# Attention and a SwiGLU FFN in one kernel: unit 2's transposes moved, a two-tile start of block 1, w_out loaded in thirds

## The chip, the cores and the metric

The kernel runs on one core of one Trainium2 chip. The metric is the device time of one execution in microseconds; lower is better. All profile times are microseconds from the start of the profiled span.

## The reference

Sliding-window attention with ALiBi biases on 8 batches, 8 heads, 576 positions and a head width of 64, followed by an FFN on the 4608 x 512 result:

```python
scores = scale * np.matmul(q, k.transpose(0, 1, 3, 2))
bias = slopes[:, None, None] * (-np.abs(rel).astype(np.float32))[None, :, :]
mask = (rel >= 0) & (rel < 128)
scores = np.where(mask, scores + bias[None], -1000000000.0)
attn = np.exp(scores - np.max(scores, axis=-1, keepdims=True))
attn = attn / (np.sum(attn, axis=-1, keepdims=True) + 1e-09)
x = np.matmul(attn, v)         # then heads side by side: (4608, 512)
g = x @ w_gate                 # (512, 1536)
silu = g * (1.0 / (1.0 + np.exp(-g)))
out = (silu * (x @ w_val)) @ w_out
```

## The kernel before

**Attention units.** Two batches form a superblock; each superblock has nine units of 128 rows, the ninth made of the last 64 rows of both. For a unit the kernel transposes the rows of q and k on TensorE (`transposed`; the names are `pt` for the PSUM tile, `kn` and `qn` for the loaded rows), computes transposed scores (`ps` at L282; `psc` at L318 for the narrow ones), takes the exponential on ACT (`ex`, `exc`), multiplies with a mask on DVE, and forms the weighted sums `av` with a column of ones beside v, which gives the denominators (L350). DVE then divides: a reciprocal `rec` (L353) and a product `x` (L354), in two halves of four heads. `x_transposed` turns x on TensorE into `px` (L377) and a copy takes it to `xT`, the FFN's moving operand: on DVE for units 0 to 3 (L379), on ACT later (L381). The transposes of the first units share one PSUM buffer, tag "po"; later ones use the four buffers of tag "a", which scores and sums use as well.

**FFN blocks.** Nine blocks of 512 rows, four units each (the last is made of the ninth units). For each of twelve groups m of 128 hidden columns, `wide` computes `pg` and `pv` (L403) in three PSUM buffers of tag "gv". `gate` makes `tt` on ACT (L421) and `uu` on DVE (L422); `val` makes `hT` on DVE (L433). `wide` can be begun on the first tiles of a block: `begin(n, tiles, block)` computes the first n products of a block on the columns that are there, and the later call does the rest. `project` multiplies block 0's `hT` with `wo_sb` (`po`, L457), from the last group, m = 11, down to m = 0, in four sets of twelve matmuls. From block 1 on the output product uses a seven-product scheme, for which DVE makes sums of w_out (`T`, L481 to L484) and of hT (`S`, L491 to L494).

**Order.** The first four units (`first_tiles`) and the first FFN steps are written out by hand for TensorE, DVE and ACT. After that a scheduler orders the instructions by priority and its own estimate of time, until step 60, when TensorE's order is fixed again; `tc.high_priority()` puts instructions ahead. Each engine executes its list in order. The passage from block 0 to block 1, where unit 6 is divided and transposed and scores for units 7 and 8 are made, lies in the scheduled part.

**Loads.** All loads but the first are issued on POOL in an order written out by hand at the end of the kernel. They cast from 32 to 16 bits. POOL's loads use eight completion semaphores in turn, so a load is issued once the load eight places earlier has landed. `load_qk` loads 128 KB for each of k and q, `load_v` 128 KB of v, in two halves of 64 KB for a ninth unit; `load_w(c0, c1)` loads 256 hidden columns of each of w_gate and w_val; wo_sb (12 x 128 rows of 512) is loaded in two halves, rows 6 to 11 first.

Of the kernel before, what the change touches and what calls it, by code (L numbers as in the profile page):

```python
# [50 lines left out]
def kernel(  # L51
# [10 lines left out]
    nc = tc.nc  # L62
# [127 lines left out]
    def load(rank):  # L190
        load_qk(rank)
        load_v(rank)
# [137 lines left out]
    def weighted(i):  # L330

        s, p = units[i]
        x = xpool.tile([P, H, D], FP16, name="x", tag="x")
        xs[i] = x
        for half in range(2):
            pool, tag = (ps_f, "gv") if i < FIRST else (ps_a, "a")
            av = pool.tile([P, 4, D + 1], FP32, name="av", tag=tag)
            todo = []
            for j in range(4):
                h = 4 * half + j  # L340
                if p == 8:
                    for n, kt in enumerate((3, 7, 8)):
                        todo.append((j, ex[(s, "c", n)][:, slot(h), :], va[9 * s + kt][:, h, :]))
                else:
                    if p not in (0, 4):
                        todo.append((j, ex[(s, p - 1)][:, slot(h), 128:256],
                                     va[9 * s + p - 1][:, h, :]))
                    todo.append((j, ex[(s, p)][:, slot(h), 0:128], va[9 * s + p][:, h, :]))
            for n, (j, w, val) in enumerate(todo):
                nc.tensor.matmul(av[:, j, :], w, val, start=(n == 0), stop=(n == len(todo) - 1))  # L350
            rec = xpool.tile([P, 4, 1], FP32, name="rec", tag="rec", bufs=4)
            with tc.high_priority() if i == 7 else ExitStack():
                nc.vector.reciprocal(rec, av[:, :, D:D + 1])  # L353
                nc.vector.tensor_mul(x[:, 4 * half:4 * half + 4, :], av[:, :, 0:D],  # L354
                                     rec.broadcast_to([P, 4, D]))
# [8 lines left out]
    def x_transposed(i):  # L364
        n, j = place(i)
        if n not in xT:
            xT[n] = bpool.tile([P, NKB, 512], FP16, name="xT", tag="xTc" if n == 8 else "xT",
                               bufs=1 if n == 8 else 3)
        x = xs.pop(i).rearrange("p h d -> p (h d)")
        dst = xT[n][:, :, j * P:(j + 1) * P]  # L370
        if i >= X_DMA_FROM:
            nc.sync.dma_start_transpose(dst, x)
            return
        pool, tag, n = (ps_f, "po", 1) if i < FIRST else (ps_a, "a", 4)
        pt = pool.tile([P, NKB, P], FP16, name="px", tag=tag, bufs=n)
        for kb in range(NKB):
            nc.tensor.transpose(pt[:, kb, :], x[:, kb * P:(kb + 1) * P], idm if i < FIRST else idm2)  # L377
        if i < FIRST:
            nc.vector.tensor_copy(dst, pt)  # L379
        else:  # L380
            nc.scalar.copy(dst, pt)  # L381
# [325 lines left out]
    def ffn():  # L707

        for n in range(NBLK):
            if n > 1:  # L710
                parts = chain(strassen(n - 1, 0), strassen(n - 1, 1))
            if n == 1:
                begin(3, 3, 1)
                for j in range(PRE):
                    for _ in project(0, j, ps_f, "po", 1):
                        yield 1.0
            if n == SEVEN_FROM:
                break
            due, given = 0, 0
            for m in range(NMB):  # L720
                for half, _ in enumerate(gate_val(n, m)):
                    scored[0] = False
                    yield 1.0
                    due += n > 1 and 2 * m + half in AT
                    while due and not (scored[0] and given % 7 == 1):
                        next(parts)
                        due, given = due - 1, given + 1
                        yield 0.75
                    if n > 1:
                        for _ in range(1 + (len(later) > 3)):  # L730
                            if later:
                                later.pop(0)()
                if n == 1:
                    if m in (4, 6, 8, 10):
                        for _ in project(0, m // 2 - 2, ps_f, "po", 1):
                            yield 1.0
                    if m in (4, 6, 8):
                        weight_sums(m // 2 - 2)
                if n > 0 and m >= 9:
                    (at_once if n == 1 and m < 11 else later.extend)(sums(n, m - 9))  # L740
                if n + 1 == SEVEN_FROM:
                    if m == SILU_AT:
                        attention_ends()
                        by_silu.update((n, i) for i in range(m + 1, NMB))
                    if m in (SILU_AT + 1, SILU_AT + 2):
                        later.extend(gate_val_weight_sums(m - SILU_AT - 1))
                    if m == SILU_AT:
                        later.extend(x_sums(n + 1))
            if n > 1:
                assert next(parts, 0) == 0  # L750
        ends = [strassen(NBLK - 1, t) for t in range(2)]
        tail = ExitStack()
        for n, k, name, which in seven_steps():
            if k == 0 and n > SEVEN_FROM:
                assert next(parts, 0) == 0
                parts = chain(strassen(n - 1, 0), strassen(n - 1, 1))
            if n == SEVEN_FROM and k in (1, 3, 10, 17):
                later.extend(gate_val_weight_sums(2 + (k + 4) // 7))
            yield 0.5
            if k % 3 == 2 and k < 42:  # L760
                next(parts)
                yield 0.75
            if k == 20 and n + 1 < NBLK:
                later.extend(x_sums(n + 1))
            if k == 35:
                later.extend(sums(n, 0))
            if name == "fourth" and which is not None and which[1] > 3:
                if n + 1 < NBLK or k < 39:
                    later.extend(sums(which[0], which[1] - 3))
            for _ in range(2 if len(later) > 4 or k < 7 else 1):  # L770
                if later:
                    later.pop(0)()
            if n == NBLK - 1 and k == 38:
                at_once(later)
                later.clear()
                tail.enter_context(tc.manual_schedule(engines={ET.DVE}))
            if n == NBLK - 1 and k == 39:
                one, two = sums(n, 1), sums(n, 2)
                one[0]()
            if n == NBLK - 1 and k == 41:  # L780
                one[1]()
                next(ends[0])
                yield 0.75
            if n == NBLK - 1 and k == 42:
                two[0]()
        assert next(parts, 0) == 0 and not later
        at_once((two[1], one[2], two[2], one[3], two[3]))

        for t in (1, 0, 1, 0, 1, 0, 1, 0, 0, 1, 0, 1, 1):
            next(ends[t])  # L790
            yield 0.75
        tail.close()
# [28 lines left out]
    def begin(n, tiles, block=0):  # L821

        for m, which in ((0, "g"), (0, "v"), (1, "g"), (1, "v"), (2, "g"), (2, "v"))[:n]:
            if early.get((block, m, which), (None, 0))[1] < tiles * P:
                wide(block, m, which, tiles * P)

    def first_tiles():

        first_masks()
        transposes_to(need[0])  # L830
        for n, _ in enumerate(run(scores(0))):
            if n == 0:
                transposes_to(need[1])
        for i in range(FIRST):
            if i + 1 < FIRST:
                for n, _ in enumerate(run(scores(i + 1))):
                    if n == 0 and i + 2 < FIRST:
                        transposes_to(need[i + 2])
            else:
                later_masks()  # L840
            weighted(i)
            if 0 < i < FIRST - 1:
                x_transposed(i - 1)
        begin(4, 2)
        x_transposed(2)
        x_transposed(3)
        begin(4, 3)

# [36 lines left out]
            nc.gpsimd.dma_start(dst[:, :, c0:c1], src[:, :, c0:c1])  # L885


    queue = ExitStack()
    queue.enter_context(tc.manual_schedule(engines={ET.Pool}))
    load_qk(1, "qk")  # L890
# [19 lines left out]
    load_qk(7, "qk")  # L910
    load_v(6)
    load_w(1280, 1536)
    load_v(7)
    load(8)
    load_qk(9)
    load_qk(10, "q")
    nc.gpsimd.dma_start(wo_sb[:, 6:12, :], wo2[:, 6:12, :])
    nc.gpsimd.dma_start(wo_sb[:, 0:6, :], wo2[:, 0:6, :])
    load_v(9)
    load_qk(10, "k")  # L920
    load_v(10)
# [94 lines left out]
```

The softmax here doesn't subtract the row's maximum and nothing guards it: scores larger than these inputs give would overflow.

## Time and profile before

| what | value |
|---|---|
| three timed runs | 338.82, 339.06, 339.23 us (median 339.06) |
| profiled run: device time, span of the core | 339.0 us, 337.2 us |
| TensorE matmuls / weight loads | 328.0 us / 217.8 us busy |
| DVE / ACT / POOL | 274.3 / 208.0 / 109.8 us busy |
| loads by POOL (q0) | 18.62 MB as written |
| granted TensorE clock | full throughout |

A busy time adds the stretches in which at least one instruction of the engine ran. In the timeline a row gives the start, the duration, the engine, the line, the operation with its operands and how many instructions were merged into the row; in brackets stands the idle time before it and what ended it. Rows named PEld are weight loads, which run beside matmuls. "DMA" in a bracket is a transfer that landed.

### The profile page before, as it was taken

How to read it: one execution, taken by the hardware profiler on the slowest of the kernel's cores; microseconds unless marked ns; L12 is line 12 of the kernel's file. 1: busy time of each engine (PE TensorE's matmuls, PEld its weight loads, DVE VectorE, ACT ScalarE, POOL GpSimd, SP SyncE). 2: the span in 40 equal slices, each digit the busy share in tenths (PEclk: the TensorE clock that was granted, in tenths of full speed). 3: DMA queues.
4: the chain of work that ended last, by engine and by line, in shares of the span. 5: the costliest groups of instructions: out<-in, count | busy, mean ns of one | idle time of the engine just before them, and what ended most of it. 6: DMA issues, size and time to landing. Idle time of an engine off the chain costs nothing.

```text
span 337.2 us, 7693 instructions
## 1 busy us (share of the span) xinstructions
PE 328.0 (97%) x2947; PEld 217.8 (65%) x2947; DVE 274.3 (81%) x643; ACT 208.0 (62%) x415; POOL 109.8 (33%) x136
## 2 busy tenths in 40 slices
PE   8999989999999999999999999999999999999994
PEld 4564445454455665656655655666788888888884
DVE  4668877998798679998899999999855885775683
ACT  4866775565675766656656557463467667776650
POOL 8977682295783372665217000000000000000000
PEclk9999999999999999999999999999999999999999
DMA  9999999999999999999999952031101101011014
GB/s 151 169 178 179 166 101 190 141 112 162 140 160 136 175 132 127 178 153 168 151 184 156 135 106 78 18 64 47 65 0 64 62 2 65 3 62 64 0 64 125
DMA packets 160037, 37.37 MB, mean 111 GB/s; under 512 B 147328, under 2 KB 155648, under 8 KB 160000
## 3 DMA queue, kind: packets, MB, share of 16 engines
q0 software_dynamic: 118336, 18.62, 87.7%
q1 hardware_dynamic: 40976, 17.64, 30.0%
q10 hardware_dynamic: 688, 0.62, 0.6%
q8 instruction: 23, 0.38, 0.5%
q14 instruction: 14, 0.11, 0.1%
HBM read 37.91 MB, written 9.44 MB: 140 GB/s over the span
## 4 chain that ended last, share of the span: by engine, by line
PE 83%; DMA 8%; DVE 3%; POOL 2%; ACT 1%; issue 1%; DVEq 0%; POOLq 0%
PE po L538 19%; PE pv L403 15%; PE pg L403 15%; PE gX L627 9%; PE gY L627 5%; PE av L350 4%; DMA wo_sb<-in_moe_w_out_dram 4%; PE ps L282 4%; PE p L538 3%; PE po L457 3%; DMA va<-in_v_dram 3%; PE gZ L627 2%; DMA qn<-in_q_dram 2%; PE px L377 1%; PE psc L318 1%
## 5 line engine op out<-in xcount | busy, mean ns | idle before, releaser
L403 PE MATMUL pv<-xT,wv_sb 128*128 128x512 f16 (+3 forms) x308 | 76.1, 365 | 1.0 <-DVE uu L422 0.9
L403 PE MATMUL pg<-xT,wg_sb 128*128 128x512 f16 (+3 forms) x312 | 76.0, 363 | 0.3 <-DVE xT L379 0.2
L421 ACT ACTIVATE tt<-pg 128x512 f16<-128x512 f32 x68 | 40.9, 603 | 46.7 <-PE pg L403 46.7
L288 ACT ACTIVATE ex<-ps 128x512 f16<-128x512 f32 x96 | 50.0, 606 | 7.6 <-PE ps L282 7.6
L422 DVE SCALAR_TENSOR_TENSOR uu<-tt,pg 128x512 f16<-128x512 f16 x67 | 45.5, 679 | 9.3 <-ACT tt L421 9.1
L433 DVE TENSOR_TENSOR hT<-uu,pv 128x512 f16<-128x512 f16 x68 | 46.1, 679 | 2.8 <-PE pv L403 1.3
L181 POOL DMA_DIRECT2D va<-in_v_dram x40 | 34.3, 862 | 32.3 <-PE av L350 22.6
L538 PEld LDWEIGHTS <-hT 128*128 128x128 f16 x384 | 37.2, 98 | 10.6 <-issue 0.8
L403 PEld LDWEIGHTS <-wv_sb 128*128 128x128 f16 x308 | 27.5, 98 | 25.0 <-issue 3.5
L403 PEld LDWEIGHTS <-wg_sb 128*128 128x128 f16 x312 | 27.8, 98 | 22.9 <-issue 1.9
L187 POOL DMA_DIRECT2D qn<-in_q_dram x39 | 33.4, 864 | 21.3 <-DMA va<-in_v_dram 9.8
L187 POOL DMA_DIRECT2D kn<-in_k_dram x39 | 33.5, 860 | 19.1 <-DMA qT<-qn 6.4
L538 PEld LDWEIGHTS <-S 128*128 128x128 f16 x288 | 27.4, 98 | 7.3 <-issue 1.4
L294 DVE TENSOR_TENSOR ex<-ex,m_reg 128x1024 f16<-128x1024 f16 x42 | 28.6, 684 | 2.4 <-ACT ex L288 2.3
L354 DVE TENSOR_TENSOR x<-av,rec 128x256 f16<-128x256 f32 x72 | 28.6, 418 | 0.4
L538 PE MATMUL po<-T,S 128*128 128x256 f16 x192 | 25.9, 273 | 0.3 <-ACT u2s L564 0.3
L538 PE MATMUL po<-T,hT 128*128 128x256 f16 x192 | 26.0, 272 | 0.0
L322 ACT ACTIVATE exc<-psc 128x512 f16<-128x512 f32 x40 | 21.3, 607 | 1.9 <-PE psc L318 1.9
L681 DVE TENSOR_TENSOR hT<-s,v 128x512 f16<-128x512 f16 x18 | 7.6, 423 | 17.7 <-ACT s L680 17.7
L350 PEld LDWEIGHTS <-ex 128*128 128x128 f16 x384 | 17.4, 97 | 4.1 <-issue 0.7
L350 PE MATMUL av<-va,ex 128*128 128x65 f16 x384 | 19.3, 193 | 0.1
L282 PE MATMUL ps<-qT,kT 64*128 64x256 f16 x192 | 16.9, 272 | 0.1
(130 smaller groups left out, 533.8 us busy)
## 6 DMA issues: line engine op xcount, KB each, us to landing
out_dram<-osb SPq DMA_DIRECT2D x32, 256.0 KB, 2.3
va<-in_v_dram POOLq DMA_DIRECT2D x32, 128.0 KB, 9.0
qn<-in_q_dram POOLq DMA_DIRECT2D x31, 128.0 KB, 8.2
kn<-in_k_dram POOLq DMA_DIRECT2D x31, 128.0 KB, 9.0
wg_sb<-in_moe_w_gate_dram POOLq DMA_DIRECT2D x6, 256.0 KB, 7.7
wv_sb<-in_moe_w_val_dram POOLq DMA_DIRECT2D x6, 256.0 KB, 8.3
wo_sb<-in_moe_w_out_dram POOLq DMA_DIRECT2D x2, 768.0 KB, 11.2
kn<-in_k_dram POOLq DMA_DIRECT2D x8, 64.0 KB, 8.1
```

The costliest lines, as they stand in the source:

```text
L181: nc.gpsimd.dma_start(va[rank][p0:p1, :, 0:D], src)
L187: nc.gpsimd.dma_start(t_[p0:p1], src)
L282: nc.tensor.matmul(two[par][:, j, :], kT[rows, ks, pair, :], qT[rows, p:p + 2, pair, :], start=(j == 0 and not early_tile), stop=(j == 1))
L288: nc.scalar.activation(e[:, o:o + 2, :], banks[q4][par], AF.Exp, scale=scale)
L294: nc.vector.tensor_mul(e[:, o, :], e[:, o, :], reg[:, o, :])
L350: nc.tensor.matmul(av[:, j, :], w, val, start=(n == 0), stop=(n == len(todo) - 1))
L403: nc.tensor.matmul(ps[:, c0:c1], w[:, kb, ms], xT[n][:, kb, c0:c1], start=(kb == 0 and c0 == 0), stop=(kb == NKB - 1 and c1 == 512), skip_ ...
L421: nc.scalar.activation(tt, pg[:, c0:c1], AF.Tanh, scale=0.5)
L422: nc.vector.scalar_tensor_tensor(out=uu, in0=tt, scalar=one if (n, m) == PIN else 1.0, in1=pg[:, c0:c1], op0=ALU.add, op1=ALU.mult)
L433: nc.vector.tensor_mul(hT[n][:, m, c0:c1], acted[(n, m)][1][:, c0:c1], pv[:, c0:c1])
L538: nc.tensor.matmul(dst, a[:, m, cols], b[:, m, :], start=(start and m == 0), stop=(m == HM - 1), skip_group_check=True)
L627: nc.tensor.matmul(dst[:, i, :], w[:, kb, c0 + i * P:c0 + (i + 1) * P], a[:, kb, :], start=(start and i == 0 and kb == 0), stop=(i == 1 an ...
```

## The change

Four edits, all of order:

1. In `first_tiles` the transposition of unit 2's x is put ahead of `begin(4, 2)`, the first FFN products of block 0; before, it followed them.
2. At the start of block 1, `begin(2, 2, 1)` is put ahead of `begin(3, 3, 1)`: the first pg and pv of block 1 are begun on two tiles (units 4 and 5), and continued on the third (unit 6) by the call after it.
3. The divisions of unit 6 get the priority that unit 7's have.
4. On POOL, wo_sb is loaded in three parts of four rows (8 to 11, 4 to 7, 0 to 3) instead of two of six, and rank 8 is loaded as k and q first, v later.

```diff
-            with tc.high_priority() if i == 7 else ExitStack():
+            with tc.high_priority() if i in (6, 7) else ExitStack():
                 nc.vector.reciprocal(rec, av[:, :, D:D + 1])
...
             if n == 1:
+                begin(2, 2, 1)
                 begin(3, 3, 1)
...
                 x_transposed(i - 1)
+        x_transposed(2)
         begin(4, 2)
-        x_transposed(2)
         x_transposed(3)
         begin(4, 3)
...
+    def load_wo(m0, m1):
+        nc.gpsimd.dma_start(wo_sb[:, m0:m1, :], wo2[:, m0:m1, :])
...
     load_w(1280, 1536)
+    load_qk(8)
+    load_wo(8, 12)
     load_v(7)
-    load(8)
+    load_wo(4, 8)
     load_qk(9)
     load_qk(10, "q")
-    nc.gpsimd.dma_start(wo_sb[:, 6:12, :], wo2[:, 6:12, :])
-    nc.gpsimd.dma_start(wo_sb[:, 0:6, :], wo2[:, 0:6, :])
+    load_v(8)
+    load_wo(0, 4)
     load_v(9)
     load_qk(10, "k")
     load_v(10)
```

In the built program, TensorE's order differs from the one before in two places only: at the edit in `first_tiles`, and from the passage between blocks 0 and 1 to the sums of unit 9. DVE's and ACT's differ from unit 6's divisions to the first sums S of block 1.

## The prediction

> **What bounds the kernel now.** I read the page first, then TensorE's timeline stretch by stretch, then the DVE timeline and the transfer rates where it has gaps. The page, and the chain of waits:
>
> ```profile
> PE 328.0 (97%) x2947; PEld 217.8 (65%) x2947; DVE 274.3 (81%) x643; ACT 208.0 (62%) x415; POOL 109.8 (33%) x136
> ...
> 45.58 13.21 DMA wo_sb<-in_moe_w_out_dram
> ```
>
> TensorE sets the end, but 97% hides gaps: ends of matmuls are modelled and overlap. I measure a gap as the distance between two starts less the streaming time, 0.216 us for 512 columns (four take 0.86 in the chain), 0.109 for 256, 0.055 for 128. So counted, TensorE idles some 14 us up to 105 us, and under 4 us after that, mostly the tail. Three places bear on the change.
>
> ```profile
> 18.91 0.39 PE L377 MATMUL px<-idm,x 128*128 128x128 f16 x4
> 19.82 0.38 PE L377 MATMUL px<-idm,x 128*128 128x128 f16 x4 [0.52 <-DVE xT L379]
> ...
> 31.78 0.23 PEld L214 LDWEIGHTS <-qn 128*128 128x128 f16 x4 [0.17 <-DMA qn<-in_q_dram]
> ```
>
> Place A: the transposes of units 2 and 3 share one PSUM buffer ("po"), so the second waits for the first one's copy: 0.91 - 0.22 = 0.69 us. But at 31.79 TensorE waits for a load, q of rank 6, issued at 23.49 and landing 8.2 us later.
>
> ```profile
> 46.33 0.38 PE L403 MATMUL pv<-xT,wv_sb 128*128 128x512 f16 x1
> 47.27 0.29 PE L377 MATMUL px<-idm,x 128*128 128x128 f16 x2 [0.57 <-DVE x L354]
> ...
> 48.21 0.28 PE L377 MATMUL px<-idm,x 128*128 128x128 f16 x2 [0.20 <-DVE x L354]
> ...
> 49.17 0.38 PE L318 MATMUL psc<-qT,kT 64*128 64x128 f16 x7 [0.20 <-ACT xT L381]
> ...
> 60.30 1.02 PE L403 MATMUL pv<-xT,wv_sb 128*128 128x512 f16 x4 [0.66 <-DVE uu L422]
> ```
>
> Place B: the passage from block 0 to block 1. TensorE waits for x of unit 6, then for exps. From 46.33 to unit 8's weighted sum (65.14) are 18.81 us.
>
> ```profile
> 58.90 0.75 DVE L481 SCALAR_TENSOR_TENSOR T<-wo_sb,one 128x512 f16<-128x512 f16 x1 [0.77 <-DMA wo_sb<-in_moe_w_out_dram]
> ```
>
> Place C: DVE stands before the second half of wo, which lands at 58.79; the uu queued behind it delays the pv at 60.30 (gap 0.84). The rates say why wo is late (columns as in the page: busy times, clock, DMA share, GB/s):
>
> ```profile
> 42.00:45.00 3.00, 3.00 (x21) 1.43 (x20) 2.90 (x8) 1.61 (x4) 2.09 (x4) 1.00 1.72 83
> 45.00:49.00 4.00, 3.16 (x49) 1.87 (x48) 3.40 (x9) 3.07 (x6) 4.00 (x6) 1.00 1.28 86
> ...
> 50.00:56.00 6.00, 5.94 (x69) 4.07 (x67) 4.39 (x10) 4.21 (x9) 2.56 (x3) 1.00 1.23 204
> 56.00:60.00 4.00, 3.63 (x19) 1.48 (x18) 3.23 (x8) 1.25 (x3) 0.88 (x1) 1.00 2.26 161
> ```
>
> For 7 us the transfers run at half rate. In the built order each POOL load waits on one of eight semaphores in turn, so for the load eight earlier; here six of the eight in flight are 64 KB halves.
>
> [...] here wo (2 KB rows) runs at 204 GB/s and q, k, v (256-byte rows) at some 155. [...]
>
> **The change part by part**, on the clock of the trace before.
>
> Transposing x of unit 2 first. It still waits for the "po" buffer until unit 1's copy ends (17.11), when the FFN products start in any case: transposes 17.17 to 17.39, four products of 0.435 to 19.13. Its copy runs on DVE after x of unit 3 (about 18.13 to 18.55), so unit 3's transposes go at 19.13 without a wait and the next products at 19.35 instead of 20.04: 0.69 us saved. Nothing is added. But the order up to 46.33 is otherwise unchanged, and q of rank 6 still lands at 31.69, since loads are issued on POOL against earlier loads. TensorE arrives 0.69 earlier and waits 0.69 longer. Bounds: 0 to 0.7. I take 0.1, for DVE and ACT having cleared a little more.
>
> Two tiles of block 1 first, and the priority. The built order puts a 256-column pg and a quarter of pv ahead of unit 6's transposes, and both x of unit 6 ahead of the exc product on DVE, which saves its second half 0.59. Splitting columns costs nothing (4 x 0.109 + 4 x 0.055 is 4 x 0.164). The exc product slips 0.34 and hides behind the 1.06 that DVE waits for exps at 50.14. I walk the new order with durations of the trace. After the pv at 46.33 the 256-column products run to 47.09; x is there at 47.27 (gap 0.18); k, then x again (0.05), q, the rest of pv to 48.31; the third tile needs ACT's copy of unit 6 (48.60, gap 0.29); the products to 49.37; 16 score products to 50.03. ACT starts their exps at 49.9, 0.51 apart, later than before (49.01), so the last scores wait 0.35 and 0.18 for banks, and unit 7's sums 0.14 and 0.05; seven po matmuls now lie among them, as wo rows 8 to 11 and 4 to 7 are there. Small waits 0.06 and 0.07 follow. The first groups of m=1 end at 55.30, scores of unit 9 at 55.85, and there stands the ninth po matmul, which needs wo rows 0 to 3. With them there, pv waits for uu of m=0 (0.41) and pg for hT (0.34), waits that five po matmuls at 54.57 cover now. The rest streams, and unit 8's sum begins at 63.49. The work is 15.04 us in both, twelve po matmuls included: the gaps fall from 3.77 to 2.12, a gain of **1.65 us**. T goes behind two uu-hT pairs, so place C is gone.
>
> wo in three parts. The k8, q8 halves take the places of v7, wo rows 8 to 11 are issued near 37.1, rows 4 to 7 near 39.4, then k9 at 41.2 as before. From 41.0 until 58.8 the one-us rates sum to 2,577 KB, 1,573 of them wo; with no bubble, 1,573/205 + 1,004/155 = 14.2 us, so rows 0 to 3 land near **55.2**, just ahead of 55.85. Ahead of them q10 lands near 52, wanted at 53.9; v7 near 47, wanted at 51.6; v8 near 53, wanted at 63.5. One more POOL issue costs 0.85 us while POOL waits for semaphores anyway; SP gets the same transposes in the same order.
>
> Afterwards. DVE has no gap from 58.90 to 80.6 before. In the new order it stands idle about 2.7 us in 46 to 58 instead of 3.3, so at L494's S, where the orders meet, it is only 0.6 earlier; but then it waits 0.96 for unit 10's sum today, so it can follow by 0.6 + 0.96 = 1.56. Sums of T and S are put off, not the gates. Later loads wait for TensorE (22.6 us under POOL in the table of waits), so these move with it. Sum: 0.1 + 1.65 = 1.75 us of the 337.2 us span. The profiled run took 339.0 us and the three others 338.82 to 339.23, so the span stands 1.8 us under all alike and the difference carries over: 339.06 - 1.75 = **337.3**.
>
> **Rivals.**
> 1. The passage gains, A is swallowed: 337.3. Chance 0.55.
> 2. A's 0.69 survives too, if q6 lands earlier: 339.06 - 0.69 - 1.65 = 336.7. Against it: nothing that feeds that load moves. 0.11.
> 3. DVE becomes the bound in 58 to 80, its busiest stretch, and only its 0.6 comes through: 338.5. For it: 19.8 us busy in 20. Against it: TensorE waits for DVE little there, and the deferred T. 0.17.
> 4. Not what it says: exps hold the passage and new waits eat the filled gap, 339.0. ACT is busy 3.88 of 4 us in 48 to 52. 0.06.
> 5. Slower: the ninth po matmul blocks TensorE on wo rows 0 to 3. If wo runs at the pace of its first half (786 KB in 53.9 - 47.8 = 6.1 us), the 1,573 KB take 12.2 instead of 7.7, landing 59.7. The wait of 3.9 absorbs the 0.75 of waits behind it: 3.1 lost against 1.75, so 340.4. It decides from a landing of 55.85 + 0.75 + 1.75 = 58.3 on. Against it: 204 GB/s once wo flows. 0.11.
>
> **The numbers.** A measurement of this kernel tells about 0.2%, 0.68 us, from no change. Faster: cases 1, 2 and half of 3, 0.74. Same: half of 3 and case 4, 0.15. Slower: 0.11. The range reaches from A surviving with small waits also gone (336.2) to just past case 4 (339.2).
>
> **What would show it.** Right: unit 3's transposes follow the products without a wait; a wait near 0.8 for q at 31.8; rates near 160 to 200 GB/s in 42 to 49; no DVE wait for wo; unit 8's sum near 63.4. Wrong: q6's wait not longer, or the po matmul before m=1's pv waiting for wo by over 1 us, or pg and pv waiting for uu and hT in 64 to 80.

## The result, and the profile after

The changed kernel took 337.47 us (median; 337.19 to 337.62) against 339.14 us for the kernel before, measured beside it: a ratio of 0.9951, 95% interval 0.9934 to 0.9968. A second comparison on another occasion gave 337.26 against 338.60 us, 0.9962 (0.9948 to 0.9975). So it is faster by 1.3 to 1.7 us; forecast were 1.75 and 337.3 us. The profiled span fell from 337.2 to 335.7 us.

Place A, after. TensorE's timeline and weight loads (start, duration, engine, line, operation, count, and in brackets the idle time before and what ended it):

```profile
17.30 0.38 PE L377 MATMUL px<-idm,x 128*128 128x128 f16 x4 [0.22 <-DVE xT L379]
...
19.27 0.39 PE L377 MATMUL px<-idm,x 128*128 128x128 f16 x4
...
31.90 0.23 PEld L214 LDWEIGHTS <-qn 128*128 128x128 f16 x4 [0.83 <-DMA qn<-in_q_dram]
```

Unit 3's transposes follow the products without a bracket: the wait of 0.52 that stood there is gone. At 31.9 the weight load of q waits 0.83 us for its transfer, where it waited 0.17. That load was issued at 23.47 us, against 23.49 before. TensorE arrives earlier and leaves at the same time: the transposes of k start at 30.86 instead of 31.40, those of q at 31.90 instead of 31.79.

Place B, after, in the same columns:

```profile
46.41 0.38 PE L403 MATMUL pv<-xT,wv_sb 128*128 128x512 f16 x1
46.62 0.60 PE L403 MATMUL pg<-xT,wg_sb 128*128 128x256 f16 x4
47.06 0.27 PE L403 MATMUL pv<-xT,wv_sb 128*128 128x256 f16 x1
47.36 0.29 PE L377 MATMUL px<-idm,x 128*128 128x128 f16 x2
...
50.59 0.38 PE L318 MATMUL psc<-qT,kT 64*128 64x128 f16 x4 [0.19 <-ACT exc L322]
...
51.50 0.39 PE L457 MATMUL po<-wo_sb,hT 128*128 128x512 f16 x1
...
56.53 1.02 PE L403 MATMUL pv<-xT,wv_sb 128*128 128x512 f16 x4 [0.16 <-DVE uu L422]
57.39 1.03 PE L403 MATMUL pg<-xT,wg_sb 128*128 128x512 f16 x4
...
63.23 0.89 PE L350 MATMUL av<-va,exc 128*128 128x65 f16 x24
```

The two-tile products stand between the last pv of block 0 and the transposes of unit 6. From that pv to unit 8's sum are now 16.82 us instead of 18.81. The waits that remain are short: 0.19 us for an exp at 50.59, and 0.16 for uu at 56.53. The prediction's times per matmul hold in the traces: by start distances four products of 256 columns take 0.44 us here (46.62 to 47.06), four transposes of 128 columns 0.22 (19.27 to 19.49), and in the profile before three products of 384 columns take 0.49 (51.65 to 52.14).

The loads, after: the stretches of time with busy time per engine, granted clock, DMA share and GB/s:

```profile
42.00:45.00 3.00, 3.00 (x20) 1.44 (x19) 2.90 (x8) 1.61 (x4) 3.00 (x4) 1.00 1.59 198
45.00:49.00 4.00, 3.91 (x55) 2.64 (x54) 3.40 (x9) 3.09 (x7) 2.03 (x4) 1.00 1.88 173
50.00:56.00 6.00, 5.81 (x77) 3.87 (x72) 3.81 (x10) 4.94 (x10) 4.44 (x6) 1.00 2.00 169
```

83 and 86 GB/s became 198 and 173: the bubble is filled. Rows 0 to 3 of wo, issued at 45.07, landed 10.2 us later, at 55.3; the ninth po matmul, which needs them, began at 55.98. The load eight places behind them on POOL was issued at 55.60, after a wait of 0.37 us that this landing ended.

### The profile page after: what moved, and what is told of

It reads as the page before. It is cut to its first block, busy times and chain, and to the rows that moved or that the text cites. A ratio compares the mean times of both kernels' runs of the same rounds, so it can differ in the third digit from the quotient of the medians.

```text
span 335.7 us, 7711 instructions
## 1 busy us (share of the span) xinstructions
PE 326.6 (97%) x2955; PEld 217.5 (65%) x2955; DVE 273.7 (82%) x643; ACT 208.0 (62%) x415; POOL 110.5 (33%) x137
## 4 chain that ended last, share of the span: by engine, by line
PE 69%; DVE 16%; DMA 5%; POOL 4%; issue 3%; ACT 2%; DVEq 0%; ACTq 0%; POOLq 0%
PE po L538 16%; PE pv L403 12%; PE pg L403 11%; PE gX L627 9%; PE gY L627 5%; PE av L350 3%; DVE uu L422 3%; DVE hT L433 3%; PE p L538 3%; PE ps L282 3%; DMA qn<-in_q_dram 2%; DMA wv_sb<-in_moe_w_val_dram 2%; PE gZ L627 2%; DVE ex L294 2%; PE po L457 2%
## 5 line engine op out<-in xcount | busy, mean ns | idle before, releaser
L403 PE MATMUL pv<-xT,wv_sb 128*128 128x512 f16 (+2 forms) x312 | 76.3, 363 | 0.5 <-DVE uu L422 0.4
```

The lines of the kernel that those rows point to most:

```text
L403: nc.tensor.matmul(ps[:, c0:c1], w[:, kb, ms], xT[n][:, kb, c0:c1], start=(kb == 0 and c0 == 0), stop=(kb == NKB - 1 and c1 == 512), skip_ ...
```

## The experiments

My theory: the gain comes from TensorE's gaps at the passage from block 0 to block 1, which the two-tile order fills; that order puts po matmuls so early that it needs the new loads; and edit 1 is swallowed by the load of q of rank 6. The rivals: edit 1 carries its 0.69 us itself; or the loads carry the gain; or the priority does. The built programs keep the questions apart: a change of load order leaves TensorE's, DVE's and ACT's order as it is, so each pair of kernels with the same edits 1 to 3 differs in loads alone; in the traces their matmuls stand in the same order.

Each kernel is compared with the kernel before, run beside it on the same chip:

| kernel | median, us | before, us | ratio (95% interval) |
|---|---|---|---|
| edit 1 alone | 338.39 | 338.49 | 0.9999 (0.9991 to 1.0007) |
| edits 2, 3, 4 | 337.38 | 338.49 | 0.9966 (0.9954 to 0.9978) |
| all four, q6 ahead of k6 | 336.48 | 338.49 | 0.9943 (0.9931 to 0.9955) |
| before, q6 ahead of k6 | 338.51 | 338.49 | 1.0002 (0.9994 to 1.0010) |
| edit 4 alone | 338.58 | 338.77 | 0.9994 (0.9986 to 1.0003) |
| edits 2, 3 | 341.78 | 338.77 | 1.0089 (1.0073 to 1.0106) |
| edits 2, 4 | 337.53 | 338.77 | 0.9966 (0.9953 to 0.9978) |
| all four, wo 0 to 3 three loads later | 338.76 | 338.77 | 1.0017 (1.0002 to 1.0032) |
| all four | 337.26 | 338.60 | 0.9962 (0.9948 to 0.9975) |
| edits 2, 3, 4, q6 ahead of k6 | 337.34 | 338.60 | 0.9964 (0.9951 to 0.9976) |
| all four, q6 ahead of k6, again | 336.95 | 338.60 | 0.9950 (0.9938 to 0.9963) |
| all four, wo 0 to 3 two loads later | 337.60 | 338.60 | 0.9970 (0.9959 to 0.9981) |

### Edit 1 by itself

```diff
+        x_transposed(2)
         begin(4, 2)
-        x_transposed(2)
         x_transposed(3)
```

> Only the transposes of unit 2 are moved (edit 1). Theory (the load of q of rank 6 swallows it): unit 3's transposes lose their wait and the FFN products up to 30.7 stand 0.69 us earlier, then TensorE waits 0.83 us instead of 0.17 for q at 31.8, and the rest stands where it did: 339.0 us, no change within 0.1. Rival (the 0.69 comes through): 338.4.

> The changed kernel without edit 1. Theory: as the changed kernel, 337.4 to 337.6 us, with a wait for q of 0.17 at 31.8. Rival (edit 1 carries 0.69 of the gain): 338.1.

Edit 1 alone gave 338.39 against 338.49 us, no change: a gain above 0.3 us lies outside the interval. (The rival's figure of 338.4 was met, but only because the kernel before took 338.49 us here and not 339.06. The comparison decides, not the figure.) The three other edits without it gave 1.1 us, a ratio of 0.9966, which lies inside both intervals of the changed kernel. In the profile of edit 1 alone the transposes come without a wait and the weight load of q waits longer:

```profile
19.42 0.39 PE L377 MATMUL px<-idm,x 128*128 128x128 f16 x4
...
31.77 0.23 PEld L214 LDWEIGHTS <-qn 128*128 128x128 f16 x4 [0.55 <-DMA qn<-in_q_dram]
```

The wait is 0.55 us and not 0.83, because in this profile TensorE already stood 0.28 us later ahead of the edit; q is taken up at 31.77 as before (31.78). So edit 1 does what it says and buys nothing. To show that the load is the cause, the next three kernels take it away.

### The load of q of rank 6 brought forward

```diff
     load_qk(5, "k")
-    load_qk(6)
+    load_qk(6, "qk")
```

> The changed kernel with q of rank 6 loaded ahead of k of rank 6, 0.9 us earlier. Theory: q lands near 31.0, TensorE's wait falls from 0.83 us to under 0.1 and the 0.69 of edit 1 comes through to the end: 336.8 us. Rival (DVE or ACT hold the stretch behind 31.8 and the gain is lost there): 337.4.

> The kernel before with q of rank 6 loaded ahead of k of rank 6. Theory: only the wait of 0.17 us at 31.79 goes: 338.9 us, not to be told from no change. Rival (the order of these two loads is worth 0.7 without edit 1): 338.4.

> Edits 2, 3 and 4 and the earlier load of q of rank 6, without edit 1. Theory (edit 1 and the load are worth something only together): within 0.25 us of the changed kernel, 337.3. Rival (the load alone brings what the pair brought): 336.5.

> The changed kernel with q of rank 6 ahead of k of rank 6, once more: 0.7 to 0.9 us under the changed kernel, 336.6.

The swap alone does nothing for the kernel before (338.51 against 338.49). With edits 2, 3 and 4 but without edit 1 it gives 337.34 beside 337.26 for the changed kernel. With edit 1 it gives 336.95, 0.31 us under the changed kernel in the same comparison, and in the other 336.48, 0.9 under edits 2, 3 and 4, where 336.8 was expected. So edit 1 and the swap are worth something only together, as the theory has it; the size of 0.7 to 0.9 under the changed kernel was missed. TensorE's timeline of the changed kernel with the swap (the second profile):

```profile
30.95 0.39 PE L214 MATMUL pt<-idm,kn 128*128 128x128 f16 x4
31.17 0.39 PE L214 MATMUL pt<-idm,qn 128*128 128x128 f16 x4
31.39 0.81 PE L403 MATMUL pv<-xT,wv_sb 128*128 128x512 f16 x3
32.37 0.61 PE L282 MATMUL ps<-qT,kT 64*128 64x256 f16 x8 [0.17 <-DVE qT L219]
```

q no longer waits, but the scores behind it now wait for DVE's copy of q, which stands behind an hT on DVE (31.29) and runs at 31.90. It looks as if this wait took a share of edit 1's gain, but it does not. The same kernel without edit 1 has it too:

```profile
31.41 0.39 PE L214 MATMUL pt<-idm,kn 128*128 128x128 f16 x4
...
32.83 0.61 PE L282 MATMUL ps<-qT,kT 64*128 64x256 f16 x8 [0.16 <-DVE qT L219]
```

From the transposes of k to the scores are 1.42 us in both, and 1.42 in the kernel before (31.40 to 32.82). That is also why the swap alone bought nothing: it moved the wait from the load to the copy. In the changed kernel with the old loads the stretch takes 1.83 us in the profile taken beside this one and 2.02 in the first. So the swap gives the changed kernel 0.41 us in these two profiles, where the medians differ by 0.31.

Between the two profiles above, edit 1 is the only difference in the kernels. Comparing the starts of the same matmuls, TensorE stands 0.21 us behind ahead of edit 1, 0.47 ahead after it, and still 0.47 ahead at the end of the kernel: once the load is out of the way, 0.68 of the 0.69 us come through. The medians of these two differ by only 0.39. The 0.21 us lie ahead of the edit, where the fourteen profiles on record differ by up to 0.43 us, with edit 1 and without; what sets that was not asked. This kernel is faster than the kernel before (0.9943 and 0.9950 of it) and than the changed kernel: all its five runs in the second comparison lie under all five of that kernel.

### The loads and the order taken apart

Three kernels: edit 4 alone, which is the part of the change from `load_wo` on and nothing else; edits 2 and 3 with the old loads, against the kernel before

```diff
-            with tc.high_priority() if i == 7 else ExitStack():
+            with tc.high_priority() if i in (6, 7) else ExitStack():
...
+                begin(2, 2, 1)
                 begin(3, 3, 1)
```

and edits 2 and 4, which have the second of these lines and the new loads, but the old condition of the priority.

> Only the loads of edit 4, in the order of instructions of the kernel before. Theory: rows 0 to 3 of wo land near 55.3, DVE no longer waits for them at 58.2 (0.0, 0.8 and 1.2 us in three profiles with the old loads), unit 8's sum starts at 64.5: as the fastest runs of the kernel before, 338.2 us, with little spread from run to run. Rival (the loads carry most of the gain): 337.5.

> Edits 2 and 3 with the old loads. Theory (TensorE blocks on wo in its own order): the first po matmul, wanted at 51.5, waits for rows 6 to 11 (53.9), the seventh, wanted 3.4 us before it can run, waits for row 5 (58.8); 5.5 us of waiting less some 0.5 of small waits behind it: 342.4 us. Rival (the loads are worth only DVE's wait): 338.2.

> Edits 2 and 4 without the priority of unit 6's divisions (and without edit 1). Theory: x of unit 6 comes half a microsecond later and the scheduler puts other work ahead of its transposes; all the products of block 1's third tile stand behind it: 0.2 to 0.6 over the kernel with edits 2, 3 and 4, 337.6 to 338.0. Rival (the priority does nothing): 337.4.

Edit 4 alone gave 0.2 us, within the error. DVE's T does not wait for wo in its profile:

```profile
58.45 0.74 DVE L481 SCALAR_TENSOR_TENSOR T<-wo_sb,one 128x512 f16<-128x512 f16 x1
```

I had expected the fastest time of the kernel before and little spread; the spread came (338.37 to 338.87), the 0.3 us came only in part. The wait of 0.77 that I read from the profile of before was not a fixed cost: 1.20 us in the profile of edit 1 alone, none in that of the kernel before with the swapped loads, all three with the old loads of wo. The kernel before ranged from 338.14 to 339.49 us in these comparisons, and this wait is one visible source. It can be read in the passage, from the last pv of block 0 to unit 8's sum:

| kernel | passage, us |
|---|---|
| before, its profile (wait of 0.77 for wo) | 18.81 |
| edit 1 alone (wait of 1.20) | 19.26 |
| before with q6 ahead of k6; edit 4 alone (no wait) | 18.1 each |
| all six profiles with edits 2, 3 and 4 and wo in time | 16.82 or 16.83 |
| edits 2, 4 | 16.90 |
| edits 2, 3 | 21.39 |

So in the passage the two-tile order is worth 1.28 us by itself, and the wait for wo another 0.71 in an execution like the one profiled before.

The order without the loads is 3.0 us slower. TensorE's timeline of edits 2 and 3:

```profile
54.06 0.38 PE L457 MATMUL po<-wo_sb,hT 128*128 128x512 f16 x1 [2.45 <-DMA wo_sb<-in_moe_w_out_dram]
...
57.90 0.38 PE L457 MATMUL po<-wo_sb,hT 128*128 128x512 f16 x1 [1.90 <-DMA wo_sb<-in_moe_w_out_dram]
```

Two blocking waits, at the first and the seventh po matmul, as expected; by start distances 2.63 + 2.07 = 4.70 us instead of 5.5, since the second half of wo came at 57.9 and not 58.8. Each holds up what stands behind it on TensorE: unit 7's sums start at 54.27, though the exc product made for them on DVE ended at 51.79, and the transposes of x at 58.11, though that x was there at 56.21. The passage is 4.56 us longer than with the new loads. So the loads are mainly a condition: alone they take away a wait that only some executions have, without them edit 2 costs, and with them it earns about 1.0 us more than they do (0.9994 for edit 4 alone, 0.9966 for edits 2 and 4).

The priority does nothing that can be measured: 0.9966 with it and without it, in two comparisons, and 16.90 against 16.82 us of passage. My expectation of 0.2 to 0.6 us missed. The timeline of edits 2 and 4:

```profile
47.72 0.29 PE L377 MATMUL px<-idm,x 128*128 128x128 f16 x2
47.84 0.39 PE L214 MATMUL pt<-idm,kn 128*128 128x128 f16 x4
48.06 0.39 PE L214 MATMUL pt<-idm,qn 128*128 128x128 f16 x4
48.29 0.49 PE L403 MATMUL pv<-xT,wv_sb 128*128 128x256 f16 x3
48.65 0.29 PE L377 MATMUL px<-idm,x 128*128 128x128 f16 x2
```

The second half of x comes later, but the transposes of k and q and the rest of the two-tile pv fill that time. Edit 2 had already taken the wait that the priority was to shorten. That is a reading: without the priority the scheduler also puts other matmuls at 107 of TensorE's 2955 places, so the comparison is of two built orders.

### How near the edge wo stands

Against the changed kernel, three loads later:

```diff
     load_v(8)
-    load_wo(0, 4)
     load_v(9)
     load_qk(10, "k")
     load_v(10)
+    load_wo(0, 4)
```

and two loads later:

```diff
     load_v(8)
-    load_wo(0, 4)
     load_v(9)
     load_qk(10, "k")
+    load_wo(0, 4)
     load_v(10)
```

> The changed kernel with rows 0 to 3 of wo loaded behind v of rank 9, k and v of rank 10, three loads of 0.9 us. Theory: they land near 58.0 instead of 55.3, the ninth po matmul waits 2.0 us for them, 0.3 of that takes the place of the wait for uu behind it: 339.1 us, 1.7 over the changed kernel. Rival (other work hides the landing): 337.4.

> The changed kernel with rows 0 to 3 of wo behind v of rank 9 and k of rank 10, two loads of 0.9 us. Theory (the ninth po matmul blocks TensorE from a landing of 55.9 on, one for one): they land near 57.1, a wait of 1.2 us of which 0.3 takes the place of another, 0.9 over the changed kernel, 338.3. The granted clock, which fell to half for some 3 us behind the wait of 2.1 us in the profile of the kernel with three loads ahead, stays full in all runs. Rival (the wait is not the cause, but what else the later load collides with): over 339.

With two loads ahead, rows 0 to 3 came 0.54 us too late by the bracket, not 1.2:

```profile
56.52 0.38 PE L457 MATMUL po<-wo_sb,hT 128*128 128x512 f16 x1 [0.54 <-DMA wo_sb<-in_moe_w_out_dram]
```

The gap is 0.60 by start distances, and the gap of 0.33 before the next pv is gone: 0.27 by this count, 0.34 us measured (337.60 - 337.26). The price holds, one for one less what it replaces; the landing was 0.6 us earlier than I had put it. I had expected a full clock in all runs, and it was full in six of seven (means of 0.997 to 1.0): one took 556.42 us at a mean granted clock of 0.559. The ratio leaves it out. It has no trace, nothing else on record is like it, and whether the later load has to do with it stays open.

With three loads ahead the profile has the expected wait, and something more. Its timeline:

```profile
58.02 0.59 PE L457 MATMUL po<-wo_sb,hT 128*128 128x512 f16 x1 [2.12 <-DMA wo_sb<-in_moe_w_out_dram]
58.39 1.91 PE L403 MATMUL pv<-xT,wv_sb 128*128 128x512 f16 x4
```

The same kernel's stretches of time, columns as above:

```profile
58.00:62.00 4.00, 3.98 (x11) 1.47 (x11) 1.65 (x3) 0.20 (x1) 0.00 (x0) 0.58 2.35 152
62.00:66.00 4.00, 4.00 (x20) 1.84 (x19) 3.71 (x8) 1.52 (x3) 1.80 (x3) 1.00 0.61 107
```

Behind the wait the granted clock (the third figure from the right) is 0.58 for 4 us, and the pv takes 1.91 us instead of 1.03. The runs of this kernel fell in two groups, 338.23 to 339.30 us (14) and 340.69 to 341.20 (6); the profiled run is of the second, so the first group shows the price of the wait alone: its middle, 338.6, is 1.1 to 1.5 us over the changed kernel by the ratios, where 1.7 was expected.

## Why the prediction was right

**Edit 1, taken at 0.1 of 0.69.** Right, and shown three ways: nothing alone, nothing missing without it, and a gain once the load that swallows it is brought forward. Rival 2 falls.

**The passage, 1.65 us.** The walk put unit 8's sum at 63.49; it began at 63.23, 1.91 us earlier than before, though the passage was entered 0.08 later: 1.99 us of gain. Gaps forecast at 0.18, 0.29, 0.35 and 0.41 measured 0.19, 0.23, 0.37 and 0.33. One step was wrong: the wait of 0.34 of pg for hT, which I derived from the PSUM buffers taken in turn, did not exist; the pg at 57.39 follows the pv directly, and 1.65 + 0.34 are the 1.99. hT of m=0 cannot have been written by then (DVE starts the two hT at 56.99 and needs 0.68 for one), so that pg had another buffer, and the one of m=1, free once uu ended at 57.08, is the only candidate I see; that is argued, not tried. The credit was also misplaced: I counted the priority as part of the passage, and it is worth nothing that could be measured.

**Place C.** Its size was taken from one profile as if it were fixed. It varies with the landing of wo between executions, and the prediction's 3.77 us of gaps contains it at 0.84. Of the 1.99 us, 0.71 are this wait and 1.28 the order. That is one reason why the gain reads 1.67 us in one comparison, 1.34 in another, and 1.11 for edits 2, 3 and 4 in a third.

**The loads.** Forecast 55.2 for rows 0 to 3, measured 55.3. Rival 5 named the right place: the bracket in the kernels with wo later is exactly that wait, and edits 2 and 3 without the loads are the slow case, by the same mechanism with the halves of wo. It did not decide because rows 0 to 3 landed at 55.3 us, not at the 59.7 that the pace of the first half gave.

**Afterwards.** DVE was said to allow no more than 1.56 us of the 1.65. It began L494's S 0.44 us earlier (79.82 against 80.26), not 0.6, and TensorE's lead shrinks there: of the 1.91 us at 63.2, 1.49 are left at unit 10's second transposes,

```profile
82.56 0.28 PE L377 MATMUL px<-idm,x 128*128 128x128 f16 x2 [0.24 <-DVE x L354]
```

which wait for a division on DVE and stood at 84.05 before. The first product of block 6 starts 1.63 us earlier (239.14 against 240.77). So rival 3 was a real limit, which took some 0.3 us of the lead. Rival 4, exps that eat the gap, left 0.37 and a few tenths and no more.

**The sum.** It came out better than its parts. The passage gave 0.34 us more than forecast, the stretch behind it lost 0.28 again (1.91 to 1.63), and edit 1 gave nothing instead of 0.1. That the first two nearly cancel is luck; that the gain sits in the passage, and not in edit 1 or in the loads alone, is not.

## What to carry to other kernels

Before pricing a gap in front of the bounding engine, look on that engine for the next wait on something that doesn't move with the work: a transfer whose issue stays where it was (here 23.49 and 23.47 us) returned none of the time saved ahead of it, the wait growing from 0.17 to 0.83 us, and nearly all of it (0.68 of 0.69 us) once that load was brought forward too. A wait that is taken away can stand up again one step later: without edit 1 the earlier load only let the scores wait for DVE's copy instead, 1.42 us from the transposes of k to the scores in either order of the loads. A matmul used as filler brings its operands' deadline with it (waits of 2.45 and 1.90 us for wo with the old loads); an order that fills gaps and the loads that make it possible have to be judged together, since either alone was worth nothing or cost 3 us. A wait on a transfer seen in one profile is a sample, 0.0 to 1.20 us in the profiles with the old loads of wo, and a kernel with a margin of 0.7 us at a blocking load is near an edge: with that load two places later the wait was 0.54 us, three places later 2.12.

## What the runs showed that I had not expected

With rows 0 to 3 of wo three loads later, a wait of 2.12 us on TensorE was followed in the profile by a granted clock of 0.58 from 58 to 62 us. By start distances the four pv behind the wait took 1.71 us (58.39 to 60.10) and the four pg after them 1.50 (60.10 to 61.60); the next four pv took 0.87. 6 of 20 runs of that kernel lie some 2 us above the rest, and these six have mean clocks of 0.993 to 0.995, the other fourteen 0.997 to 1.0.

A wait of this length does not always bring the clock down. The kernel with edits 2 and 3 had waits of 2.45 and 1.90 us in its profile at a mean clock of 0.999, and the four po matmuls at 54.97, just behind the first wait, took the 1.02 us that four matmuls of 512 columns take at full clock (1.02 and 1.03 in the timelines above). With two loads ahead the wait was 0.54 us and the mean clock of the profile 0.997. What decides whether the clock falls was not shown; no run was made to find it.
